# An attention and gated-MLP kernel whose order is computed by a planner: other durations, another margin and a table of priority shifts

## The chip, the cores and the metric

The kernel runs on one core of a Trainium2 chip, as one launch. The metric is the device time of that launch in microseconds (us); lower is better. Before the change it was 821.54 us, the median of three runs (820.73 to 823.94). The core's engines are called PE (matrix multiply; PEld is its weight load), ACT, DVE, POOL and SP. SP issues all the transfers (DMAs) of this kernel.

## What is computed

Attention with a causal mask and a bias from running sums, then a gated MLP (gMLP) block with a residual, for 8 batches of 576 tokens, 8 heads of 64, all in float32. `x` of the MLP is the attention's result with its heads side by side (512 wide), `w_in` is 512 x 1024, and `u` and `v` are the two halves of `h`:

```python
scores = scale * np.matmul(q, k.transpose(0, 1, 3, 2))
s_pos = np.maximum(s, 0.0)
cum = np.cumsum(s_pos, axis=-1)
bias = -(cum[:, :, :, None] - cum[:, :, None, :])
scores = np.where(causal, -1000000000.0, scores + np.minimum(bias, 0.0))
scores = scores - np.max(scores, axis=-1, keepdims=True)
attn = np.exp(scores)
attn = attn / (np.sum(attn, axis=-1, keepdims=True) + 1e-09)
return np.matmul(attn, v).astype(np.float32)
...
h = x @ w_in
c = np.float32(np.sqrt(2.0 / np.pi))
h = 0.5 * h * (1.0 + np.tanh(c * (h + 0.044715 * h ** 3)))
...
v_n = (v - mu) / np.sqrt(var + 1e-06) * g_ln
v_s = np.einsum('ts,bsd->btd', w_sg, v_n) + b_sg[None, :, None]
gated = u * v_s
return (x + gated @ w_out).astype(np.float32)
```

## The kernel before, in words

**The work.** There are 64 heads (8 per batch). A head's scores `sc` are formed on PE in five blocks of query rows. DVE adds the mask and takes the row extremes `mn` (an ISA instruction in the listings), ACT takes the exponentials into tiles `p`, PE transposes `p` into a PSUM bank `pt`, and PE multiplies the result with V into `xx` (and a 64-column rest into `x`). From head 8 on for the scores, and from head 12 on for V, each float32 operand is split into a high and a low part in a faster PE format (`pah` and `pal`, `pbh` and `pbl`, `pdh` and `pdl` for the transposed probabilities; `k`, `q`, `vs`, `xs`, `vn`, `gt` and the weights `wi`, `ws`, `wo` likewise). ACT copies the high part out of the bank, and DVE or POOL subtracts it to give the low part. After every second head the row sums are inverted (`rs`), transposed, written to DRAM (`rd`) and read back spread over the partitions (`rb`); POOL multiplies `xr` with them.

**The MLP of a batch** is cut into units: five `v` units (512 columns each, tile `vm` in PSUM; the fifth has 64 rows), eight `u` units (288 columns, `um`), eight `s` units (`sm`) and eight `o` units (`om`). A `u` unit's bank is read by the gelu: ACT, DVE, ACT, DVE in turn. A `v` unit's bank is held longer: gelu, then statistics (`bs`), then one more DVE pass into `vt`. The `vm`, `um`, `sm` and `om` tiles share three PSUM banks; `sc` has two, `pt` (with `x`) two, `xx` one. The MLP of batch b runs beside the attention of batch b+1. The last batch's MLP runs alone. The weights come in as 64-bit words and are put together from their bits during the first 150 us (`wraw`, `wbits`).

**What sets the order.** The kernel's functions emit nothing. They record each operation with a key (its place in units of one head, from the table `POS`). `graph` (L242) finds what each operation depends on. `plan` (L308) is a list scheduler: over and over it takes, of all engines, the ready operation that can start first by its assumed times, and among those of one engine that could start equally soon the one with the lowest key. Its assumed times come from `cost` (L189), from `LATENCY` per pair of engines plus `MARGIN` for each handover to an operation that depends on the result, from `OVERLAP` per engine, and from `ISSUE` per DMA on SP. `cost` also returned two flags, `wide` (DVE, operands in SBUF alone) and `lock` (POOL): the planner kept a wide DVE operation and a locking POOL operation apart in its assumed time. `emit` (L275) then writes the program, each engine's queue in exactly the planned order. On the chip an engine executes its queue strictly in that order, and waits where an operand or a buffer isn't there yet; the planned times themselves are not kept.

All instructions stand under one line of the source (L289, the call in `emit`; L362 in the changed kernel), so the views are read by tile names.

Of the kernel before, what the change touches and what calls it, by code (L numbers as in the profile page):

```python
# [10 lines left out]
F32R = mybir.dt.float32r  # L11
# [3 lines left out]
AF = mybir.ActivationFunctionType  # L15
# [10 lines left out]
CH = S // 2  # L26
# [145 lines left out]
class Program:  # L172
    def __init__(self, nc):
        self.ops, self.key, self.late, self.gate = [], 0.0, 0.0, None
        for name, n in METHODS.items():
            setattr(self, name, Engine(self, getattr(nc, name), n))
# [9 lines left out]
        return len(self.ops) - 1  # L186


    def cost(self, op):  # L189
# [5 lines left out]
        wide = lock = False  # L195
        d, load = 50.0, 0.0
        if e == PE:
            if name == "transpose":
                d, load = 110.0, 0.44 * ins[0].columns()
            else:  # L200
                w, m = ins
                load, n = 0.84 * w.columns(), m.columns()
                d = 0.463 * n if m.dtype == F32R else max(0.833 * n, load) + 0.833 * n
        elif e == ACT:
            f = kw.get("func")
            d = (195 if not any(ps) else 166) + 0.834 * n
            if f == AF.Exp:
                d = 480 + 0.834 * n
            elif f == AF.Tanh:
                d += 10  # L210
        elif e == DVE:
            d = 150 + 1.045 * n
            if name == "tensor_tensor_reduce":
                d += 7
            elif name == "reciprocal":
                d = 170
            elif name == "bn_stats":
                d = 687
            elif name == "bn_aggr":
                d = 172  # L220
            elif name == "memset":
                d = 60 + 0.8 * n
            elif n > 1 and not ops_ and not any(ps):
                wide = True
                if len(big) == 1:
                    d = 140 + 0.53 * n
        elif e == POOL:
            lock = n > 64
            if name == "tensor_tensor":
                d = (560 if kw["op"] == ALU.pow else 193) if n == 1 else 170 + 2.17 * n  # L230
            elif name == "tensor_scalar":
                d = 255 + 0.84 * n if n > 4 else 210
                if kw["op0"] == ALU.max:
                    d, lock = 3.3 * n, False
            else:
                d, lock = 140 + n, False
# [69 lines left out]


def plan(cost, pre, first, uses, order, bufs, prio, after, slack=(0, 0, 0, 0, 0), window=48):  # L308

    n = len(cost)
    left = [len(p) for p in pre]
    succ = [[] for _ in range(n)]
    for i, p in enumerate(pre):
        for q in p:
            succ[q].append(i)
    issue = [[] for _ in range(n)]
    for i, qs in after.items():  # L320
# [41 lines left out]
    held = asked = (0.0, 0.0)  # L362
    seqs = [[] for _ in range(5)]
    for _ in range(n):
        best = None
        for e in range(5):
            cand, least = [], 1e18
            for pr, i in ready[e][:window]:
                if e == PE:
                    s = max(pest + peocc, max(at[i], pest) + cost[i][2])  # L370
                    soon = pest + peocc + 1
                else:
                    s = max(at[i], free[e])
                    soon = free[e]
# [12 lines left out]
        del ready[e][bisect_left(ready[e], (pr, i))]  # L387
        _, d, load, wide, lock = cost[i]
        if e == PE:
            pest, peocc, end = s, d, s + d + 60  # L390
            free[e] = s
        elif e == SP:

            moved = max(moved, s + 1300) + d
            free[e], end = s + load, moved + 600
        else:
            if e == DVE and wide and held[0] <= s < held[1]:
                s = held[1]
            if e == POOL and lock and asked[0] <= s < asked[1]:
                s = asked[1]  # L400
            end = s + d
            if wide:
                asked = (s, end)
            if lock:
                held = (s, end)
# [20 lines left out]
def tile_attn_gmlp(  # L426
# [12 lines left out]
    nc = Program(tc.nc)  # L439
# [63 lines left out]
    sp = moe.tile([P, 5, 2, BH], F32R, name="sp", tag="vn", bufs=4)  # L503
# [61 lines left out]
    wo = const.tile([P, NC, 2, DM], F32R, name="wo")  # L565
    ws = const.tile([P, NT, 2, S], F32R, name="ws")
# [29 lines left out]
    wide = w_in.dtype != F32  # L596
# [43 lines left out]
    xr = {}  # L640
# [376 lines left out]
    sc, tr, pp = (scores, {}), (transposes, {}), (pv, {})  # L1017
# [90 lines left out]
```

## Time and profile before

| | |
|---|---|
| time, median of 3 runs | 821.54 us |
| the profiled execution's own time | 821.75 us |
| its span (first to last instruction) | 820.0 us |
| busy share PE, PEld, DVE, ACT, POOL | 96%, 84%, 75%, 70%, 61% |
| chain that ended last, by engine | PE 83%, DVE 7%, ACT 3%, DMA 3%, issue 3% |
| mean granted PE clock | 0.997 |
| DMA | 98.91 MB, 45.7% of the 16 engines' span |

The profile is of one execution. An instruction's row gives start, length, engine, operation, tiles and, in square brackets, how long the engine stood idle before it and what ended that. Matmuls are pipelined: each is shown with its whole passage, so that PE is counted as busy across small gaps. What a matmul costs PE is read from the distance between starts, as the chain view lists it (several matmuls of one tile merged, with their sum). "Busy" of DVE, ACT and POOL can be read directly.

### The profile page before, as it was taken

How to read it: one execution, taken by the hardware profiler on the slowest of the kernel's cores; microseconds unless marked ns; L12 is line 12 of the kernel's file. 1: busy time of each engine (PE TensorE's matmuls, PEld its weight loads, DVE VectorE, ACT ScalarE, POOL GpSimd, SP SyncE). 2: the span in 40 equal slices, each digit the busy share in tenths (PEclk: the TensorE clock that was granted, in tenths of full speed). 3: DMA queues.
4: the chain of work that ended last, by engine and by line, in shares of the span. 5: the costliest groups of instructions: out<-in, count | busy, mean ns of one | idle time of the engine just before them, and what ended most of it. 6: DMA issues, size and time to landing. Idle time of an engine off the chain costs nothing.

```text
span 820.0 us, 16771 instructions
## 1 busy us (share of the span) xinstructions
PE 791.2 (96%) x5129; PEld 687.4 (84%) x5129; DVE 614.2 (75%) x1845; ACT 574.1 (70%) x1576; POOL 497.2 (61%) x767
## 2 busy tenths in 40 slices
PE   7999989999999999999999999999999999999998
PEld 4455557999988998899988998889988998889998
DVE  5798489877797678875788677976788767884662
ACT  4777679867787577876687677875778866872350
POOL 3676679584467555585476745675555854746442
PEclk9999999999999999999999999999999999999999
DMA  7576754555425654354535554256443546321101
GB/s 226 160 222 164 173 158 112 128 136 141 115 65 132 165 129 117 88 137 111 148 93 130 137 128 119 68 128 170 122 120 89 138 113 152 85 51 44 43 8 59
DMA packets 75566, 98.91 MB, mean 121 GB/s; under 512 B 27298, under 2 KB 43876, under 8 KB 75476
## 3 DMA queue, kind: packets, MB, share of 16 engines
q1 hardware_dynamic: 75476, 97.84, 45.7%
q8 instruction: 41, 0.67, 0.4%
q14 instruction: 49, 0.40, 0.2%
HBM read 51.71 MB, written 9.90 MB: 75 GB/s over the span
## 4 chain that ended last, share of the span: by engine, by line
PE 83%; DVE 7%; ACT 3%; DMA 3%; issue 3%; POOL 1%; SPq 0%; ACTq 0%; POOLq 0%; DVEq 0%
PE sm L289 13%; PE om L289 13%; PE sc L289 12%; PE vm L289 12%; PE xx L289 11%; PE um L289 10%; PE pt L289 10%; DVE p L289 2%; ACT p L289 1%; DMA raw<-in_kq 1%; PE x L289 1%; DVE u L289 1%; DVE bs L289 1%; DVE vm L289 1%; DVE vt L289 1%
## 5 line engine op out<-in xcount | busy, mean ns | idle before, releaser
L289 ACT ACTIVATE p<-p,mn 128x320 f32<-128x320 f32 (+4 forms) x320 | 177.8, 557 | 42.3 <-DVE mn L289 38.9
L289 PE MATMUL pt<-ident,p 128*128 128x128 f32 x768 | 156.6, 276 | 4.7 <-ACT pal L289 1.4
L289 DVE CUSTOM_DVE_ANT_0 p<-sc,mask 128x448 f32<-128x448 f32 (+4 forms) x320 | 125.2, 421 | 25.4 <-PE sc L289 22.9
L289 PE MATMUL sc<-k,q 66*128 66x288 f32 (+9 forms) x672 | 134.5, 307 | 2.2 <-DMA k<-cum 1.3
L289 PE MATMUL sm<-ws,vn 128*128 128x288 f32 x768 | 134.2, 304 | 2.3 <-DVE u L289 2.3
L289 PE MATMUL um<-xs,wi 128*128 128x288 f32 x768 | 132.0, 306 | 1.4 <-DVE u L289 1.1
L289 PE MATMUL om<-gt,wo 128*128 128x288 f32 x768 | 131.0, 307 | 0.0
L289 PE MATMUL vm<-wi,xs 128*128 128x512 f32 (+1 forms) x416 | 126.8, 408 | 0.1
L289 PEld LDWEIGHTS pt<-ident,p 128*128 128x128 f32 x768 | 97.6, 140 | 28.5 <-issue 5.6
L289 PEld LDWEIGHTS sm<-ws,vn 128*128 128x128 f32 x768 | 112.2, 188 | 6.3 <-DVE u L289 4.9
L289 PEld LDWEIGHTS um<-xs,wi 128*128 128x128 f32 x768 | 110.7, 189 | 4.2 <-DVE vt L289 2.1
L289 PEld LDWEIGHTS sc<-k,q 128*128 128x128 f32 (+3 forms) x672 | 101.4, 181 | 13.1 <-DVE mn L289 3.7
L289 PEld LDWEIGHTS om<-gt,wo 128*128 128x128 f32 x768 | 109.3, 189 | 1.1
L289 POOL TENSOR_TENSOR k<-raw,k 128x576 fp32r<-128x576 f32 x56 | 80.3, 1434 | 32.0 <-ACT k L289 19.7
L289 POOL TENSOR_TENSOR gt<-u,gt 128x288 fp32r<-128x288 f32 x64 | 50.8, 808 | 57.9 <-ACT gt L289 55.8
L289 PEld LDWEIGHTS vm<-wi,xs 128*128 128x128 f32 (+1 forms) x416 | 71.2, 185 | 10.8 <-DVE vt L289 0.4
L289 DVE SCALAR_TENSOR_TENSOR u<-u,um 128x288 f32<-128x288 f32 x128 | 56.5, 441 | 10.5 <-ACT u L289 10.2
L289 POOL TENSOR_SCALAR bs<-bs 128x1 f32<-128x1 f32 (+1 forms) x80 | 17.2, 215 | 77.3 <-DVE bs L289 74.1
L289 ACT CAST pbh<-pt 128x512 fp32r<-128x512 f32 x104 | 49.4, 481 | 19.5 <-PE pt L289 18.5
L289 POOL TENSOR_SCALAR p<-p 64x64 f32<-64x64 f32 x128 | 32.2, 252 | 49.4 <-ACT p L289 36.7
L289 POOL TENSOR_TENSOR xr<-xr,rb 128x576 f32<-128x576 f32 x32 | 46.1, 1441 | 24.0 <-DMA rb<-rd 20.6
L289 ACT ACTIVATION_READ_ACCUMULATOR p<-p,mn 128x1 f32 (+1 forms) x320 | 60.2, 188 | 0.0
(123 smaller groups left out, 1645.5 us busy)
## 6 DMA issues: line engine op xcount, KB each, us to landing
q<-k SPq DMA_DIRECT2D x168, 144.0 KB
raw<-in_kq SPq DMA_DIRECT2D x56, 288.0 KB
vr<-in_vp SPq DMA_DIRECT2D x52, 192.0 KB
rb<-rd SPq DMA_DIRECT2D x64, 144.0 KB
out_t<-ot SPq DMA_DIRECT2D x64, 144.0 KB
k<-k SPq DMA_DIRECT2D x56, 144.0 KB
wraw<-in_w_in SPq DMA_DIRECT2D x16, 256.0 KB
kf<-in_kq SPq DMA_DIRECT2D x8, 288.0 KB
```

The lines of the kernel that those rows point to most:

```text
L289: r = getattr(op["eng"].real, op["name"])(*[f(a) for a in op["args"]], **{k: f(v) for k, v in op["kw"].items()})
```

## The change

Only the planner's assumptions and the keys change; the recorded operations are the same ones. The core of the diff:

```diff
-MARGIN = 100.0
-ISSUE = 450.0
+MARGIN = 36.0
+ISSUE = 550.0
+SHIFT = {
...
+    "act activation u 128x288 um": -6.17,
...
+    "dve tensor_tensor pal 128x512 pt": -3.4,
...
+}
 class Program:
...
+    def kind(self, op):
...
     def cost(self, op):
...
             if name == "transpose":
-                d, load = 110.0, 0.44 * ins[0].columns()
+                d, load = 110.0, 0.84 * ins[0].columns()
...
             if f == AF.Exp:
-                d = 480 + 0.834 * n
+                d, gap = 480 + 0.834 * n, -107
+            elif n == 512 and f == AF.Copy:
+                d = 715
...
             elif name == "bn_stats":
-                d = 687
+                d, gap = 687, 118
...
             elif n > 1 and not ops_ and not any(ps):
-                wide = True
-                if len(big) == 1:
-                    d = 140 + 0.53 * n
+                d = 155 + 1.62 * n if len(big) > 1 else 250 + 0.8 * n
...
-        return e, d, load, wide, lock
+        return e, d, load, gap
 def plan(...):
...
         elif e == SP:
-
+            if len(flight) >= 8:
+                s = max(s, flight[-8])
             moved = max(moved, s + 1300) + d
             free[e], end = s + load, moved + 600
+            flight.append(end + 1060)
         else:
-            if e == DVE and wide and held[0] <= s < held[1]:
-                s = held[1]
-            if e == POOL and lock and asked[0] <= s < asked[1]:
-                s = asked[1]
             end = s + d
...
-            free[e] = end - OVERLAP[e]
+            free[e] = end - OVERLAP[e] + gap
...
-    prio = [(op["key"], n) for n, op in enumerate(nc.ops)]
+    prio = [(op["key"] + SHIFT.get(nc.kind(op), 0.0), n) for n, op in enumerate(nc.ops)]
```

`kind` names an operation by engine, operation, output tile, shape and first input. `SHIFT` has 52 such names; its numbers, from -6.17 to 4.5, are added to the key, and one unit is one head. `gap` lengthens or shortens the time for which an engine is taken. `flight` lets the planner's SP wait for the eighth DMA before.

What this does to the queues is shown at three places. The numbers in names such as `k_5862` are buffer numbers.

**Place 1: PE, batch 3, where its first `sm` matmuls stand.** `xx<-pah` needs the high part `pah`, which ACT copies from the bank that the last `pt` of `p_3`, `p_2`, `p_1` and `p_4` filled. Before:

```order
L289 MATMUL um<-xs,wi 128x288 x7
L289 MATMUL sc<-k_5862,q_5872 128x448
L289 MATMUL sc<-k_5876,q_0_90 128x448
L289 MATMUL sc<-k_5862,q_5872 64x64
L289 MATMUL sc<-k_5876,q_0_90 64x64
L289 MATMUL pt<-ident,p_4_255 128x128 x2
L289 MATMUL sc<-k_5862,q_5872 128x320
L289 MATMUL sc<-k_5876,q_0_90 128x320
L289 MATMUL sc<-k_5862,q_5872 128x192
L289 MATMUL sc<-k_5876,q_0_90 128x192
L289 MATMUL xx<-pah,vs 128x512
L289 MATMUL sm<-ws,vn 128x288 x4
```

Now, at the same place, where the first of the two `p_3` transposes ends the first bank:

```order
L362 MATMUL pt<-ident,p_3_129 128x128 x2
L362 MATMUL pt<-ident,p_2_126 128x128
L362 MATMUL pt<-ident,p_4_276 128x128
L362 MATMUL um<-xs,wi 128x288 x11
L362 MATMUL pt<-ident,p_2_126 128x128
L362 MATMUL pt<-ident,p_4_276 128x128
L362 MATMUL um<-xs,wi 128x288
L362 MATMUL sc<-k_5832,q_5851 128x288
L362 MATMUL sc<-k_5844,q_0_90 128x288
L362 MATMUL pt<-ident,p_3_129 128x128
L362 MATMUL pt<-ident,p_4_276 128x128
L362 MATMUL xx<-pah,vs 128x512
```

Twelve `um` matmuls, two `sc` and seven transposes stand between the bank's end and its use, where one transpose and four `sc` stood.

**Place 1 on DVE**, beside those matmuls. `pal` and `pbl` belong to attention; `vt`, `vm` and `bs` with 64 rows are the fifth `v` unit; `u` is gelu. Before:

```order
L289 RECIPROCAL rs<-rs 128x10
L289 SCALAR_TENSOR_TENSOR vt<-vt,vm 64x512
L289 SCALAR_TENSOR_TENSOR u_6005<-u_6005,um 128x288
L289 ISA p_3_124,mn<-sc,mask 64x64
L289 ISA mn 64x1
L289 TENSOR_TENSOR pal<-pt,pah 128x512
L289 TENSOR_TENSOR pbl<-pt,pbh 128x512
L289 SCALAR_TENSOR_TENSOR vm<-vt,vm 64x512
L289 SCALAR_TENSOR_TENSOR u_6072<-u_6072,um 128x288
L289 BN_STATS bs<-vm 64x6
L289 TENSOR_TENSOR pbl<-pt,pbh 128x256
L289 TENSOR_TENSOR pdh<-pt,pdh 64x64 x2
```

Now:

```order
L362 TENSOR_TENSOR pal<-pt,pah 128x512
L362 TENSOR_TENSOR pbl<-pt,pbh 128x512
L362 TENSOR_TENSOR vm<-vm,vt 64x512
L362 ISA p_4_198,mn<-sc,mask 128x288
L362 ISA mn 128x1
L362 SCALAR_TENSOR_TENSOR u_6085<-u_6085,um 128x288
L362 TENSOR_TENSOR pbl<-pt,pbh 128x256
L362 ISA p_2_120,mn<-sc,mask_86 128x320
L362 ISA mn 128x1
L362 SCALAR_TENSOR_TENSOR vt<-vt,vm 64x512
L362 SCALAR_TENSOR_TENSOR u_6085<-u_6085,um 128x288
L362 TENSOR_TENSOR pdh<-pt,pdh 64x64 x2
```

`pal`, both `pbl` and `pdh` stood among the fifth `v` unit's passes, with `bs` ahead of the last of them; now `pal` and `pbl` stand ahead of that unit's first pass, and its statistics behind `pdh`.

**Place 2: PE, some 10 us later in the same batch**, where the next `sm` unit needs a bank that a `um` unit (12 matmuls) has to give back. Before:

```order
L289 MATMUL um<-xs,wi 128x288 x4
L289 MATMUL pt<-ident,p_2_122 128x128
L289 MATMUL sc<-k_5862,q_5872 128x288
L289 MATMUL sc<-k_5876,q_0_90 128x288
L289 MATMUL um<-xs,wi 128x288 x7
L289 MATMUL pt<-ident,p_1_196 128x128
L289 MATMUL um<-xs,wi 128x288 x3
L289 MATMUL pt<-ident,p_2_122 128x128
L289 MATMUL um<-xs,wi 128x288
L289 MATMUL pt<-ident,p_4_198 128x128 x2
L289 MATMUL sm<-ws,vn 128x288 x5
```

Now:

```order
L362 MATMUL sc<-k_5991,q_6007 128x192
L362 MATMUL sc<-k_6005,q_1_101 128x192
L362 MATMUL um<-xs,wi 128x288 x10
L362 MATMUL pt<-ident,p_2_120 128x128
L362 MATMUL pt<-ident,p_4_198 128x128
L362 MATMUL um<-xs,wi 128x288 x2
L362 MATMUL xx<-pah,vs 128x512
L362 MATMUL xx<-pal,vs 128x512
L362 MATMUL xx<-pbh,vs 128x448
L362 MATMUL pt<-ident,p_3_122 128x128
L362 MATMUL pt<-ident,p_4_198 128x128
L362 MATMUL sm<-ws,vn 128x288 x3
```

Before, the `um` unit whose bank `sm` takes ended within the first row shown; now it ended ahead of all these rows, and the twelve `um` in them are a unit of their own.

**Place 3: SP, during the first 100 us**, where the next head's `raw` (K and Q) is fetched among weights (`wraw`, 256 KB each). Before:

```order
L289 DMA rb<-rd 64x576 x2
L289 DMA wraw<-in_w_out 128x512
L289 DMA xq<-xs 128x2x64 x2
L289 DMA wraw<-in_w_out 128x512 x3
L289 DMA q_1103<-k_1079 64x576
L289 DMA q_0_90<-k_1079 64x576
L289 DMA raw<-in_kq 128x576
```

Now:

```order
L362 DMA rb<-rd 64x576 x2
L362 DMA wr_972<-bh 1x16x18 x2
L362 DMA q_1058<-k_1041 64x576
L362 DMA q_0_90<-k_1041 64x576
L362 DMA wraw<-in_w_out 128x512
L362 DMA raw<-in_kq 128x576
L362 DMA q_1058<-k_1054 64x576
L362 DMA wst<-in_w_sgt 64x288
L362 DMA wraw<-in_w_out 128x512 x2
```

`raw` stood behind four `wraw`, three of them in a row; now one `wraw` stands ahead of it, and the pair follows it.

More of the change, by code (lines that the diff above doesn't have):

```diff
@@ L63 @@
 PE, ACT, DVE, POOL, SP = range(5)
+UNITS = ("pe", "act", "dve", "pool", "sp")
 METHODS = {"tensor": PE, "scalar": ACT, "vector": DVE, "gpsimd": POOL, "sync": SP}
@@ L67 @@
 OVERLAP = [0, 93, 75, 25, 0]
-MARGIN = 100.0
-ISSUE = 450.0
+MARGIN = 36.0
+ISSUE = 550.0
+SHIFT = {
+    "act activation p__ 128x192 p__": 3.23,
+    "act activation p__ 128x320 p__": 1.06,
+    "act activation p__ 128x576 p__": 1.07,
+    "act activation p__ 64x64 p__": 0.73,
+    "act activation u 128x288 um": -6.17,
+    "act activation wbits 128x256 wraw": -1.92,
+    "act copy k 128x576 raw": 3.54,
+    "act copy pah 128x512 pt": -2.55,
+    "act copy pal 128x512 pt": -1.51,
+    "act copy pdh 64x64 pt": 0.17,
+    "act copy vs 128x384 vr": 1.01,
+    "act copy xr 64x64 x": -0.9,
+    "dve bn_aggr bs 128x2 bs": -1.68,
+    "dve bn_stats bs 64x6 vm": 0.81,
+    "dve scalar_tensor_tensor u 128x288 u": -2.54,
+    "dve scalar_tensor_tensor vm 128x512 vt": 0.46,
+    "dve scalar_tensor_tensor vt 128x512 vt": -0.33,
+    "dve scalar_tensor_tensor vt 64x512 vt": -1.36,
+    "dve tensor_scalar wbits 128x256 wbits": -1.69,
+    "dve tensor_tensor pal 128x512 pt": -3.4,
+    "dve tensor_tensor pdl 128x192 pt": 1.12,
+    "dve tensor_tensor vm 64x512 vm": 0.64,
+    "dve tensor_tensor ws 128x288 wst": -1.4,
+    "dve tensor_tensor xr 64x64 x": 4.5,
+    "dve tensor_tensor_reduce p__ 128x192 sc": -0.27,
+    "dve tensor_tensor_reduce p__ 128x320 sc": 1.08,
+    "dve tensor_tensor_reduce p__ 64x64 sc": -5.74,
+    "pe matmul sc 128x192 q": -1.11,
+    "pe matmul sc 128x192 q_": -4.69,
+    "pe matmul sc 128x288 qf": 0.07,
+    "pe matmul sc 128x320 q": -0.05,
+    "pe matmul sc 128x320 q_": -0.69,
+    "pe matmul sc 128x448 q": -1.38,
+    "pe matmul sc 128x448 q_": -0.36,
+    "pe matmul sc 128x448 qf": -1.38,
+    "pe matmul sc 64x64 q": -0.2,
+    "pe matmul sm 128x288 vn": 0.36,
+    "pe matmul vm 128x512 xq": 0.63,
+    "pe matmul vm 128x512 xs": -0.09,
+    "pe matmul vm 64x512 xs": 0.54,
+    "pe matmul x 64x64 vf": -2.06,
+    "pe matmul xx 128x512 vs": 1.01,
+    "pe matmul xx 64x448 vf": 1.38,
+    "pe matmul xx 64x512 vf": 1.7,
+    "pool tensor_scalar wbits 128x256 wbits": 0.96,
+    "pool tensor_scalar xs 128x576 xr": -0.78,
+    "pool tensor_tensor k 128x576 raw": -1.91,
+    "pool tensor_tensor wo 128x256 wbits": 2.47,
+    "sp dma_start wraw 128x512 -": -0.25,
+    "sp dma_start wst 128x288 -": 0.87,
+    "sp dma_start wst 64x288 -": 0.87,
+    "sp dma_start xq 128x128 xs": 1.08,
+}
 class Buf:
@@ L186, in add, with name @@
         return len(self.ops) - 1
+    def kind(self, op):
+        def name(vs):
+            return "".join(c for c in vs[0].buf.name if not c.isdigit()) if vs else "-"
+        vs = op["outs"] + op["ins"]
+        dims = "%dx%d" % (vs[0].dims[0][1], vs[0].columns())
+        return " ".join([UNITS[op["eng"].n], op["name"], name(op["outs"]), dims, name(op["ins"])])
     def cost(self, op):
@@ L194, in cost @@
         ops_ = bool(outs) and outs[0].buf.pool.psum
-        wide = lock = False
-        d, load = 50.0, 0.0
+        d, load, gap = 50.0, 0.0, 0.0
         if e == PE:
             if name == "transpose":
-                d, load = 110.0, 0.44 * ins[0].columns()
+                d, load = 110.0, 0.84 * ins[0].columns()
             else:
@@ L202, in cost @@
                 load, n = 0.84 * w.columns(), m.columns()
-                d = 0.463 * n if m.dtype == F32R else max(0.833 * n, load) + 0.833 * n
+                d = 0.463 * n if m.dtype == F32R else max(0.84 * n, load) + 0.84 * n + 70
         elif e == ACT:
@@ L206, in cost @@
             d = (195 if not any(ps) else 166) + 0.834 * n
+            rows = (outs or big)[0].dims[0][1]
             if f == AF.Exp:
-                d = 480 + 0.834 * n
+                d, gap = 480 + 0.834 * n, -107
+            elif n == 512 and f == AF.Copy:
+                d = 715
+            elif n == 384:
+                gap = 115
+            elif rows == 64 and f is None:
+                gap = 95 if n == 64 else 45
             elif f == AF.Tanh:
@@ L212, in cost @@
             d = 150 + 1.045 * n
+            rows = (outs or big)[0].dims[0][1]
+            if name == "tensor_tensor" and rows == 64:
+                gap = 98 if n == 64 else 79
+            elif name == "scalar_tensor_tensor" and n == 512:
+                gap = 48
             if name == "tensor_tensor_reduce":
                 d += 7
+                gap = 60 if n == CH else 0
             elif name == "reciprocal":
-                d = 170
+                d = 202
             elif name == "bn_stats":
-                d = 687
+                d, gap = 687, 118
             elif name == "bn_aggr":
@@ L233, in cost @@
                 if kw["op0"] == ALU.max:
-                    d, lock = 3.3 * n, False
+                    d = 3.3 * n
             else:
-                d, lock = 140 + n, False
+                d = 140 + n
         else:
@@ L361, in plan @@
     pest = peocc = moved = 0.0
-    held = asked = (0.0, 0.0)
+    flight = []
     seqs = [[] for _ in range(5)]
@@ L387, in plan @@
         del ready[e][bisect_left(ready[e], (pr, i))]
-        _, d, load, wide, lock = cost[i]
+        _, d, load, gap = cost[i]
         if e == PE:
@@ L392, in plan @@
         elif e == SP:
+            if len(flight) >= 8:
+                s = max(s, flight[-8])
             moved = max(moved, s + 1300) + d
             free[e], end = s + load, moved + 600
+            flight.append(end + 1060)
         else:
-            if e == DVE and wide and held[0] <= s < held[1]:
-                s = held[1]
-            if e == POOL and lock and asked[0] <= s < asked[1]:
-                s = asked[1]
             end = s + d
[L402 to L405, printed above, removed]
-            free[e] = end - OVERLAP[e]
+            free[e] = end - OVERLAP[e] + gap
         start[i], fin[i] = s, end
```

1 line of the change is left out of this document (removed).

## Prediction

> **What bounds the kernel now.** I read the page first: busy shares, then the chain that ended last.
>
> ```profile
> PE 791.2 (96%) x5129; PEld 687.4 (84%) x5129; DVE 614.2 (75%) x1845; ACT 574.1 (70%) x1576; POOL 497.2 (61%) x767
> PE 83%; DVE 7%; ACT 3%; DMA 3%; issue 3%; POOL 1%; SPq 0%; ACTq 0%; POOLq 0%; DVEq 0%
> ```
>
> PE is the bound, and it has work almost everywhere. But matmuls overlap, so "busy" hides small gaps. The chain view gives what a matmul costs PE where nothing is waited for, and how long a batch takes.
>
> ```profile
> 72.67 0.45 PE pt L289 x4
> 284.90 1.08 PE sc L289 x8
> ...
> 666.87 1.08 PE sc L289 x8
> ...
> 770.03 2.79 PE vm L289 x12
> 772.83 3.20 PE um L289 x24
> 805.64 11.09 PE om L289 x84
> ```
>
> The same group of eight `sc` matmuls comes back once a batch, at 284.90 and, four batches on, at 666.87: a batch takes 95.5 us. A 288-column matmul costs 3.20/24 = 0.133 us (0.46 ns a column), a 512-column one 2.79/12 = 0.233, a transpose 0.45/4 = 0.113.
>
> One batch therefore needs, counted from the loops: 96 `um` + 96 `om` + 112 `sm` matmuls at 0.133 = 40.4 us; 56 `vm` at 0.233 = 13.0; 100 transposes at 0.113 = 11.3; for eight heads' scores eight narrow matmuls (1.08) and four of 288 columns (0.53), 12.9; for eight heads' `xx` and `x` 3072 columns each at 0.46 ns, 11.3. The sum is 88.9 us. So **6.6 us of each batch are lost in waits**, and 88.9 us is a floor that no order changes, as long as PE runs the same matmuls.
>
> Where are they lost? The windows of one batch show it, columns being PE, PEld, DVE, ACT, POOL:
>
> ```profile
> 412.00:420.00 8.00, 8.00 (x50) 6.91 (x49) 7.14 (x21) 6.92 (x20) 5.74 (x12) 1.00 0.32 82
> 420.00:428.00 8.00, 7.96 (x55) 7.04 (x54) 7.60 (x26) 6.84 (x20) 6.13 (x15) 1.00 0.42 95
> 428.00:436.00 8.00, 7.22 (x47) 5.89 (x47) 7.27 (x21) 6.84 (x20) 3.67 (x7) 1.00 0.10 25
> 460.00:468.00 8.00, 8.00 (x60) 7.81 (x59) 3.95 (x11) 4.14 (x11) 5.12 (x6) 1.00 0.79 226
> ```
>
> From 412 to 436 us DVE is busy for 22.0 of 24 us; at 460 it is half idle. In this bulge gelu, the `v` units' statistics and the softmax meet, and there PE loses time. The timeline of PE, and the chain inside the bulge:
>
> ```profile
> 429.44 0.75 PE L289 MATMUL sc<-k,q 128*128 128x320 f32 x4
> 430.78 0.50 PE L289 MATMUL xx<-pah,vs 128*128 128x512 f32 x1 [0.59 <-ACT pah L289]
> ...
> 435.82 0.90 PE L289 MATMUL um<-xs,wi 128*128 128x288 f32 x5
> ...
> 438.00 0.27 PE L289 MATMUL pt<-ident,p 128*128 128x128 f32 x1
> ...
> 441.05 0.93 PE L289 MATMUL sm<-ws,vn 128*128 128x288 f32 x5 [0.38 <-DVE u L289]
> ```
>
> ```profile
> 429.45 0.62 DVE p L289
> ...
> 434.85 0.36 DVE pdl L289
> ```
>
> **Place 1**, from 429.44 to 435.82, takes 6.38 us. PE runs 8128 columns of matmuls there (3.74 us) and five transposes (0.57): 2.1 us are lost. The chain runs on DVE throughout, from `p` to `pdl`. **Place 2**, from 438.00 to 441.05, takes 3.05 us for 13 matmuls of 288 columns (1.73) and five transposes (0.57): 0.75 us lost, while `sm` waits for a bank that gelu's last pass releases. These two make 2.85 of the 6.6 us.
>
> The other loss is at the start. In windows of 20 us:
>
> ```profile
> 0.00:20.00 20.00, 14.45 (x53) 9.48 (x53) 10.97 (x40) 9.25 (x26) 7.25 (x19) 1.00 0.74 229
> 80.00:100.00 20.00, 18.16 (x86) 10.91 (x86) 8.43 (x35) 12.92 (x40) 14.41 (x20) 0.91 0.72 179
> 120.00:140.00 20.00, 18.15 (x116) 14.34 (x115) 18.04 (x54) 18.78 (x51) 18.65 (x34) 1.00 0.38 90
> sum 200.00, PE 184.00 PEld 132.64 DVE 151.81 ACT 143.79 POOL 133.98; mean PE 18.40 PEld 13.26 DVE 15.18 ACT 14.38 POOL 13.40
> ```
>
> PE idles 16.0 of the first 200 us, 5.55 of them in the first 20, where it has no data yet. The remaining 10.45 us are open to a better order.
>
> **The change, part by part.** No operation is added or removed, so PE's floor stays. But lone transposes become runs, so both have to be priced. A lone one among `um` matmuls:
>
> ```profile
> 438.54 1.08 PE L289 MATMUL um<-xs,wi 128*128 128x288 f32 x7
> 439.46 0.27 PE L289 MATMUL pt<-ident,p 128*128 128x128 f32 x1
> 439.49 0.64 PE L289 MATMUL um<-xs,wi 128*128 128x288 f32 x3
> 439.97 0.27 PE L289 MATMUL pt<-ident,p 128*128 128x128 f32 x1
> ```
>
> The next `um` starts 0.03 us after it, which looks free; but the three `um` then take 0.48 us to the next transpose, 0.08 more than 3 x 0.133. Together 0.11, what a transpose in a run costs. Runs cost 0; with 800 transposes and an error of 2 ns each, 1.6 us either way.
>
> *Place 1.* The cover of `pah` is the PE work between the bank's last transpose and `xx<-pah`. Before, it is one transpose and 1024 columns, 0.58 us. Now it is twelve `um` (1.60), two `sc` (0.27) and seven transposes (0.79): 2.65 us.
>
> ```profile
> L289 ACT CAST pah<-pt 128x512 fp32r<-128x512 f32 x52 | 30.3, 583 | 13.4 <-PE pt L289 7.7 <-PE xx L289 5.5
> L289 DVE TENSOR_TENSOR pal<-pt,pah 128x512 fp32r<-128x512 f32 x52 | 35.7, 687 | 4.4 <-ACT pah L289 3.7
> ```
>
> `pah` takes 0.58 us and `pal` 0.69, so the old cover couldn't hold even an idle ACT; the new one holds both in a row. With `pal`, `pbl` and `pdh` ahead of the statistics, I take the loss here to fall from 2.1 to about 0.2. *Place 2.* Before, the bank's `um` unit ended 12 matmuls of 288 columns, two `sc` and five transposes ahead of `sm`, 2.4 us. Now the rows shown alone hold 2.9 us, and the unit ended earlier still. I take all 0.75 as gone. *The rest*, 3.75 us a batch, hangs on many short handovers; for a tenth of it, 0.35 us, the longer covers should help as well. In sum 3.0 us a batch. Its bounds: 0.75 (place 2 alone, if the bulge of place 1 only moves), and 5.1 (a rest of 1.5). From 200 to 750 us the batch repeats 550/95.5 = 5.76 times: **17.3 us**, between 4.3 and 29. After 750 us the last MLP runs alone and both orders end in a row of 84 `om`; 0.
>
> *The start.* What is late at 95 us is a fetch:
>
> ```profile
> 95.46 6.99 DMA raw<-in_kq
> ...
> 97.52 0.44 ACT L289 ACTIVATE wbits<-wraw 128x256 f32<-128x256 f32 x1 [2.87 <-DMA wraw<-in_w_out]
> ...
> 102.52 0.67 ACT L289 CAST k<-raw 128x576 fp32r<-128x576 f32 x1 [1.37 <-DMA raw<-in_kq]
> ```
>
> ```profile
> L289 PE MATMUL om<-gt,wo x768: 288/295/384, 168.0 to 816.4; 128*128 128x288 f32 x192
> ```
>
> `raw` took 7 us behind the burst of `wraw`, and ACT stood 2.87 and 1.37 us. With `raw` ahead of the burst this goes, but then a `wraw` is late, for `wo`, which the first `om` needs at 168 us (its row stands last above). Elsewhere in the start DVE is full (18.04 of 20 at 120 us), and an order can't shorten that. Of 10.45 us I take half, **5 us**; bounds 0 and 9.
>
> *Margin, issue, flight.* They show only through the order, and are in the above. On SP, `rb` now follows `rd` directly in 12 of 32 cases, in none before:
>
> ```profile
> 483.05 0.29 SPq L289 DMA_DIRECT2D rd<-rt  x1
> ...
> 486.73 1.19 SPq L289 DMA_DIRECT2D rb<-rd  x2
> ```
>
> Before, 3.7 us lay between, filled with other issues. Now SP waits for `rd` to land, up to 3.7 us, with `q`, `k` and `raw` of the next head queued behind it, and POOL's `xr` behind `rb`. I take 0, since the heads' splits stand 9 us of PE work or more ahead of their scores; if half of the 12 cost PE 1.5 us, 9 us. The Trainium skill, page "DMA: Bandwidth & Descriptors", section "Anatomy of one DMA — SWDGE (gpsimd) path", gives a fixed 2.0 us for a transfer, on another issuing path. By that, as an estimate, SP would stand 12 x 2 = 24 us in all; if PE lost every one of them, the sum below would end at 823. No row here shows the landing by itself.
>
> **Sum.** 17.3 + 5 = 22.3 us. The profiled execution took 821.75 us (span 820.0, and 1.75 around it), so 799.4; the median lies 0.2 lower, and I say **799**.
>
> **Rivals.**
>
> *The bulge moves (A).* DVE's work from 412 to 436 us is the same, and so is its 92% share; what is put ahead pushes something else behind, here the fifth `v` unit, on which later `sm` wait. Then place 2 alone is won, 4.3 us: 817. For it speaks the full DVE; against it, that DVE is half idle at 460 us and has time to catch up.
>
> *Nothing happens (B).* The waits at these places last 0.59 and 0.38 us of PE idle time by the timeline; if the 6.6 us are mostly delays that no order touches, the table moves names and not time: 820. Against it, 2.85 us sit at two places with a named cause.
>
> *Nearly all is won (C).* If 5.1 us a batch go and 9 at the start, 38 us: 783.
>
> *Slower (D): DVE and POOL collide at the start.* The old planner kept `wide` DVE and `lock` POOL operations apart; the new one doesn't, and uses mean durations.
>
> ```profile
> L289 DVE SCALAR_TENSOR_TENSOR wbits<-wraw,wbits x48: 407/423/1778, 15.2 to 150.2; 128x256 int32<-128x256 int32 x48
> L289 DVE SCALAR_TENSOR_TENSOR wbits<-wraw,wbits 128x256 int32<-128x256 int32 x48 | 27.3, 573 | 0.4
> 60.74 1.78 DVE L289 SCALAR_TENSOR_TENSOR wbits<-wraw,wbits 128x256 int32<-128x256 int32 x1
> 60.88 0.72 POOL L289 TENSOR_TENSOR wi<-wbits,wi 128x256 fp32r<-128x256 f32 x1
> ```
>
> The same operation takes 0.42 us in the median and up to 1.78, beside POOL's work; its mean is 0.57. So 48 of them lose 48 x 0.15 = 7.2 us already. With the 32 other SBUF operations of the start, 80 in all, a mean loss of 0.6 us instead of 0.15 would be 36 us of a full DVE; less the 17 us of the batches the time is 840. It decides above 0.43 us each (22.3 us in all plus what is lost now). The page "SBUF — State Buffer" of the Trainium skill, section "SBUF: two separate sides", says that DVE and GpSimd share a port pair as an exclusive lock, the loser blocked for the other's whole instruction; the row of 1.78 us agrees. By that rule each unplanned meeting costs up to one POOL operation. Against it, POOL's work is as thin as before, and the old order had meetings too.
>
> **How the numbers follow.** Forecast (790 to 811): 0.55. C (under 790): 0.10. A (812 to 817): 0.12. B: 0.14. D: 0.09. A measurement of this kernel can tell about 0.5% (4 us) from no change: faster than 817.4 are forecast, C and A, 0.77; same 0.14; slower 0.09. The range, 783 to 820, reaches over A to the middle of B, and leaves out D and the tails of B and C, under 0.2.
>
> **What would show it.** The same `sc` group should come back every 92.5 us. `xx<-pah` in the middle of a batch should show no idle time, and the idle time of PE before 200 us should be near 11. If a batch takes 94.5 us or more with a DVE chain of several us in it, A was right; if the median of the `wbits` passes rises, D. I am wrong as well if transposes in runs cost more than 0.113 us, as the floor would then rise.

## The result, and the profile after

The changed kernel takes **796.62 us** (median of 4 runs, 795.22 to 797.55), beside 822.01 us for the kernel before (820.73 to 823.94): a ratio of **0.9688, 95% interval 0.9662 to 0.9714**. The profiled execution of it took 797.55 us, with a span of 795.7, 24.3 less than before. 799 was forecast, with the range 783 to 820.

The page of the changed kernel, busy shares and the chain that ended last:

```profile
PE 778.5 (98%) x5129; PEld 689.7 (87%) x5129; DVE 616.9 (78%) x1845; ACT 576.5 (72%) x1576; POOL 492.5 (62%) x767
PE 89%; DVE 4%; ACT 2%; issue 2%; DMA 2%; POOL 1%; SPq 0%; DVEq 0%; POOLq 0%; ACTq 0%
```

PE's share of the chain rose from 83 to 89%, and DVE's fell from 7 to 4%. The busy time of DVE, ACT and POOL is within 1% of what it was. Windows of 8 us in one batch (columns PE, PEld, DVE, ACT, POOL) and one of 200 us in the middle of the kernel; the last row is that of the kernel before:

```profile
412.00:420.00 8.00, 8.00 (x55) 7.08 (x54) 7.59 (x29) 7.89 (x23) 5.65 (x10) 1.00 0.29 74
420.00:428.00 8.00, 8.00 (x61) 7.80 (x60) 7.73 (x25) 7.89 (x24) 4.57 (x10) 1.00 0.40 100
428.00:436.00 8.00, 8.00 (x62) 7.76 (x61) 7.75 (x23) 5.99 (x17) 3.43 (x9) 1.00 0.60 174
...
400.00:600.00 200.00, 199.55 (x1379) 185.99 (x1378) 163.12 (x503) 158.28 (x433) 126.29 (x196) 1.00 0.46 124
```

```profile
400.00:600.00 200.00, 196.87 (x1334) 179.24 (x1333) 155.45 (x478) 150.81 (x413) 120.13 (x184) 1.00 0.47 121
```

The bulge is still there: from 412 to 436 us DVE is busy for 23.1 of 24 us, more than the 22.0 before. But PE shows no idle time in it any more, and idles 0.45 us in 200, where 3.13 were.

For the batch period I take an operation that runs once a batch, DVE's last pass over the fifth `v` unit. First the timeline of the kernel before, then of the changed one, third and sixth batch:

```profile
346.88 0.69 DVE L289 TENSOR_TENSOR vnr<-vt,vnr 64x512 fp32r<-64x512 f32 x1
...
633.39 0.69 DVE L289 TENSOR_TENSOR vnr<-vt,vnr 64x512 fp32r<-64x512 f32 x1
```

```profile
341.77 0.69 DVE L362 TENSOR_TENSOR vnr<-vt,vnr 64x512 fp32r<-64x512 f32 x1
...
616.95 0.69 DVE L362 TENSOR_TENSOR vnr<-vt,vnr 64x512 fp32r<-64x512 f32 x1
```

A batch took (633.39 - 346.88)/3 = 95.5 us, and takes 91.7 now (91.6 from the fourth on). The same rows of all eight batches place the gain: at the second, 251.28 and 248.50, the changed kernel is 2.8 us ahead; between the second and the eighth (794.36 and 769.92) it wins 21.7; behind the eighth it loses 0.1. Together 24.3, the difference of the spans.

Place 1 of the prediction now reads so, on PE:

```profile
419.32 0.60 PE L362 MATMUL pt<-ident,p 128*128 128x128 f32 x4
419.68 1.71 PE L362 MATMUL um<-xs,wi 128*128 128x288 f32 x11
...
421.99 0.48 PE L362 MATMUL xx<-pah,vs 128*128 128x512 f32 x1
...
427.31 0.29 PE L362 MATMUL sm<-ws,vn 128*128 128x288 f32 x1
```

`xx<-pah` shows no idle time ahead of it. From 419.32 to 427.31, 7.99 us, PE runs 39 matmuls of 288 columns (5.19 us at 0.133), 3520 columns of `xx`, `x` and one `sc` (1.63) and nine transposes (1.02), by the rows between: 7.84 us. So 0.15 us are lost there, where 2.1 were. On DVE beside it, `pal` and `pbl` stand ahead of the fifth `v` unit, as in the order:

```profile
420.23 0.68 DVE L362 TENSOR_TENSOR pal<-pt,pah 128x512 fp32r<-128x512 f32 x1
420.83 0.67 DVE L362 TENSOR_TENSOR pbl<-pt,pbh 128x512 fp32r<-128x512 f32 x1
421.43 0.68 DVE L362 TENSOR_TENSOR vm<-vm,vt 64x512 f32<-64x512 f32 x1
...
426.63 0.68 DVE L362 BATCH_NORM_STATS2 bs<-vm 64x6 f32<-64x512 f32 x1
```

For place 2, the group of `sm` matmuls in one batch, before (442.3 to 537.9 us) and now (433.7 to 525.3). The last number is PE's idle time ahead of the group, and what ended it:

```profile
L289 PE MATMUL sm<-ws,vn 128*128 128x288 f32 x98 | 17.9, 306 | 0.4 <-DVE u L289 0.4
```

```profile
L362 PE MATMUL sm<-ws,vn 128*128 128x288 f32 x97 | 17.4, 303 | 0.0
```

In the start the gain came at another place than forecast. Three windows of 20 us of the changed kernel, and then the one of the kernel before that the prediction does not show:

```profile
80.00:100.00 20.00, 18.82 (x91) 12.17 (x92) 13.20 (x40) 13.56 (x41) 14.44 (x18) 0.91 0.66 172
120.00:140.00 20.00, 20.00 (x129) 16.35 (x128) 18.63 (x54) 18.41 (x51) 16.60 (x29) 1.00 0.44 118
140.00:160.00 20.00, 20.00 (x149) 19.19 (x148) 19.01 (x62) 17.35 (x50) 14.80 (x23) 1.00 0.48 120
```

```profile
140.00:160.00 20.00, 18.09 (x131) 16.83 (x130) 18.44 (x53) 16.72 (x49) 12.68 (x20) 1.00 0.50 125
```

From 120 to 160 us PE idled 3.76 us before and not at all now, although DVE is fuller there than it was. From 80 to 120 us, where `raw` was late, PE's idle time fell only from 3.6 to 2.9 us.

### The profile page after: what moved, and what is told of

The parts are those of the page before. It is cut to its first block, busy times and chain, and to the rows that moved or that the text cites. A ratio compares the mean times of both kernels' runs of the same rounds, so it can differ in the third digit from the quotient of the medians.

```text
span 795.7 us, 16803 instructions
## 1 busy us (share of the span) xinstructions
PE 778.5 (98%) x5129; PEld 689.7 (87%) x5129; DVE 616.9 (78%) x1845; ACT 576.5 (72%) x1576; POOL 492.5 (62%) x767
## 4 chain that ended last, share of the span: by engine, by line
PE 89%; DVE 4%; ACT 2%; issue 2%; DMA 2%; POOL 1%; SPq 0%; DVEq 0%; POOLq 0%; ACTq 0%
PE sm L362 15%; PE um L362 13%; PE sc L362 13%; PE xx L362 12%; PE om L362 12%; PE vm L362 12%; PE pt L362 11%; PE x L362 1%; DVE wbits L362 1%; ACT p L362 1%; DMA wraw<-in_w_in 1%; DMA k<-cum 1%; DVE p L362 1%; ACT pdh L362 0%; SPq L362 0%
## 5 line engine op out<-in xcount | busy, mean ns | idle before, releaser
L362 ACT ACTIVATE p<-p,mn 64x64 f32<-64x64 f32 (+4 forms) x320 | 178.7, 559 | 55.7 <-DVE mn L362 53.2
L362 DVE CUSTOM_DVE_ANT_0 p<-sc,mask 128x320 f32<-128x320 f32 (+4 forms) x320 | 126.0, 421 | 23.8 <-PE sc L362 21.5
L362 PE MATMUL sc<-k,q 128*128 128x288 f32 (+9 forms) x672 | 140.7, 307 | 1.3 <-DVE mn L362 1.1
L362 PE MATMUL pt<-ident,p 128*128 128x128 f32 x768 | 137.1, 275 | 3.2 <-DVE pbh L362 1.5
L362 PE MATMUL om<-gt,wo 128*128 128x288 f32 x768 | 132.9, 304 | 0.0
L362 PE MATMUL um<-xs,wi 128*128 128x288 f32 x768 | 129.7, 302 | 0.0
L362 PE MATMUL vm<-wi,xs 128*128 128x512 f32 (+1 forms) x416 | 119.5, 405 | 0.0
L362 POOL TENSOR_TENSOR vs<-vr,vs 128x384 fp32r<-128x384 f32 x52 | 53.0, 1020 | 20.2 <-ACT vs L362 16.1
L362 DVE TENSOR_TENSOR pbl<-pt,pbh 128x512 fp32r<-128x512 f32 x104 | 56.4, 546 | 6.3 <-ACT pbh L362 5.6
```

The source lines that it names most:

```text
L362: r = getattr(op["eng"].real, op["name"])(*[f(a) for a in op["args"]], **{k: f(v) for k, v in op["kw"].items()})
```

## The experiments

The theory that I started from (T): the table makes the gain, by longer covers at the handovers of the bulge. Its rivals: the durations and the margin make it (P), or the table is worth something only on the new durations (M, later N). For the start, where only 2.8 of the forecast 5 us came, they are that DVE and POOL collide (C), or that transfers hold the start (Q). "Second batch" and "period" are read from the `vnr` row as above, in the profiled execution; ratios are to the kernel before, with 95% intervals. "Clock" is the mean granted PE clock of each kernel's executions, from the lowest to the highest. "Half clock" is the time ahead of the second batch, in the profiled execution, for which that clock stood at 0.5.

| kernel | time, us | ratio | second batch at | period | clock | half clock, us |
|---|---|---|---|---|---|---|
| before | 822.0 | 1 | 251.28 | 95.5 | 0.997 to 1.0 | 3.4 |
| changed | 796.62 | 0.9688 (0.9662 to 0.9714) | 248.50 | 91.7 | 0.998 to 1.0 | 3.4 |
| no table | 823.87 | 1.0018 (0.9994 to 1.0042) | 246.07 | 96.2 | 0.994 to 1.0 | 0 |
| table alone | 822.05 | 0.9993 (0.9974 to 1.0012) | 257.55 | 94.0 | 0.994 to 0.998 | 6.8 |
| margin 100 | 801.02 | 0.9748 (0.9725 to 0.9772) | 253.18 | 91.9 | 0.996 to 0.998 | 6.8 |
| old durations | 838.03 | 1.0202 (1.0177 to 1.0228) | 259.54 | 96.5 | 0.983 to 0.995 | 3.4 |
| before, margin 36 | 837.41 | 1.0190 (1.0173 to 1.0207) | 255.51 | 97.7 | 0.994 to 0.996 | 10.2 |
| without `pah`, `pal` entries | 812.47 | 0.9886 (0.9855 to 0.9917) | 254.08 | 94.1 | 0.992 to 0.996 | 10.2 |
| `pah`, `pal` entries alone | 830.63 | 1.0100 (1.0071 to 1.0129) | 253.84 | 96.2 | 0.990 to 0.994 | 10.2 |
| without `u` entries | 814.84 | 0.9912 (0.9884 to 0.9941) | 250.00 | 94.3 | 0.992 to 1.0 | 0 |
| apartness kept | 802.91 | 0.9761 (0.9742 to 0.9781) | 252.54 | 91.7 | 0.996 to 1.0 | 0 |
| without weight entries | 798.98 | 0.9720 (0.9700 to 0.9740) | 249.75 | 91.6 | 0.998 | 3.4 |
| `wo` later | 802.87 | 0.9757 (0.9732 to 0.9782) | 249.17 | 91.8 | 0.996 to 1.0 | 0 |
| table from head 12 on | 795.85 | 0.9674 (0.9657 to 0.9692) | 246.85 | 91.6 | 0.998 to 1.0 | 0 |

The last two columns matter for the reading. In the changed kernel's trace, for instance, the granted clock is 0.50 from 82.3 to 85.7 us:

```profile
82.30:85.70 3.40, 3.40 (x8) 1.23 (x7) 0.20 (x1) 0.12 (x1) 0.84 (x1) 0.50 0.49 130
```

Each such stretch of 3.4 us can cost up to 1.7 us. The kernel before and the changed one have one each ahead of the second batch, so their difference of 2.8 us there is untouched. The starts of kernels with none or with more of them can differ by 1.7 us a stretch for this reason alone. The times have such a share, too. An estimate of it, at most, is the time multiplied by what the mean clock lacks to 1: some 10 us of the 838.03, 7 of the 830.63, 4 of the 837.41 and of the 812.47, 3 of the table alone and 2 of no table. The periods hold no such stretch, but for old durations (one; a batch without it takes 96.1). What lowers the clock no run here shows.

### The table taken out, and the table alone

```diff
-SHIFT = {
-    "act activation p__ 128x192 p__": 3.23,
...
-}
+SHIFT = {}
```

> The changed kernel with an empty table: the new durations, margin, issue time and flight limit stay. Theory T (the table carries the gain, by longer covers on PE's handovers): the batch period goes back to 94 to 96 us and the time to 812 to 824. Rival P (the durations and the margin carry it, the table is a trimming): period at most 92.5 us, time at most 803. Rival M (both are needed in part): 804 to 811.

No gain is left, as T expected, though the parts differ. The start is 5.2 us faster than before (246.07), of which up to 1.7 are the clock. The batches are 0.7 us slower each (96.2), so that 2.1 us of the lead are left at the eighth, and behind that 1.7 more go. Rival P falls.

The other way round, `SHIFT`, `kind` and the line with `prio` put into the kernel before:

> The kernel before with the table alone: old durations, margin 100, issue 450, and the old apartness of DVE and POOL. Theory T: most of the gain is there, period 91.5 to 93 us, time 797 to 806. Rival P: period 95 us or more, time 815 to 824. Rival M (the table was fitted to the new durations and is of little use without them): 806 to 815.

Nothing either, so T falls too: the time is that of P's range, the period (94.0) in nobody's. The start loses 6.3 us, up to 1.7 of them to the clock, and a batch gains 1.5. In the batch from 352.9 to 446 us `xx<-pah` still waits as in the kernel before, so the table by itself doesn't make the cover of place 1:

```profile
L353 PE MATMUL xx<-pah,vs 128*128 128x512 f32 x8 | 3.6, 450 | 0.6 <-ACT pah L353 0.6
```

The chain of waits of the same batch names transfers, which that of the changed kernel doesn't, but PE hardly stands for them: the transfer of 5.42 us ends in an idle time of 0.31.

```profile
438.29 5.42 DMA k<-k
```

```profile
443.84 0.45 PE L353 MATMUL sc<-k,q 128*128 128x448 f32 x1 [0.31 <-DMA k<-k]
```

M is what remains: the table and the new assumptions win 25 us together and, by the times, nothing each (at full clock, by the estimate above, the table alone some 3). Which of the new assumptions the table needs is narrowed down below, but not to one: the issue time and the flight limit were never tried by themselves.

### The margin, in both planners

```diff
-MARGIN = 36.0
+MARGIN = 100.0
```

> The changed kernel with the old margin of 100 ns. Theory T: the margin only shows through the order, and a larger one leaves as much cover: 792 to 801, period 91 to 92.5 us. Rival P: the smaller margin is what lets the planner pack, so the time rises to 804 or more, period 93 us or more.

801.02 us, 4.4 more than the changed kernel, at the edge of T's range. The period is the same within 0.2 us, so in a batch of the middle the margin is worth nothing, as T said. The profiled executions differ by 5.5 us. At the second batch the one with margin 100 is 4.7 us late (253.18 against 248.50), up to 1.7 of them by the clock. By the seventh 2.9 are left, and some 3 more are lost on the way to the eighth (775.87 against 769.92). So the difference stands at the start and in the last batch.

Then the margin of 36 with the old durations, with the table and the new issue time and flight limit (`cost` as before, `gap` 0, no apartness):

> The changed kernel with the old planner's durations (no gap, weight load of a transpose 0.44 ns a column); table, margin, issue time and flight limit as changed, and no apartness. Theory N (the table works only on the order that the new durations give; margin 100 and the apartness in a batch cost nothing): the batch gain falls to under 2 us, as with the table alone, time 806 to 818. Rival (issue time and flight limit are what the table alone lacked): batch gain 3.5 us or more, time 796 to 803.

838.03 us, slower than the kernel before, and outside both expectations: I had not thought that the small margin would hurt. By the trace 8.3 us are lost ahead of the second batch (259.54), and a batch without half clock takes 96.1 us, 2.1 more than with the table alone and its margin of 100. Up to 10 us of the 16 above the kernel before can be the clock. From this came the last test, the kernel before with the margin alone:

```diff
-MARGIN = 100.0
+MARGIN = 36.0
```

> The kernel before with the margin of 36 ns alone. Theory N (the old durations are too short for DVE's passes between SBUF tiles, and the margin of 100 made up for it; a small margin is usable only with the longer durations): slower, 828 to 842, as the kernel with table and margin 36 on old durations was (838). Rival (a small margin does harm only together with the table, or none at all): 818 to 825.

837.41, in N's range, and a batch takes 97.7 us, 2.2 more. The same edit thus costs 15.4 us on the old durations (up to 4 of them by the clock) and wins 4.4 on the new ones with the table. This fits that the large margin had covered what the old durations left out, but no run shows which durations these were. The diff names candidates: among others, `gap` adds 118 ns behind each `bn_stats` and 98 and 79 ns behind passes of 64 rows, which is 5 x 0.118 + 8 x (0.098 + 0.079) = 2.0 us of DVE a batch for the `v` units and the two `xr` passes of each head. The new durations were not tried one by one.

### Which entries of the table

The entries of place 1 taken out, then these entries alone, in the changed kernel:

```diff
-    "act copy pah 128x512 pt": -2.55,
-    "act copy pal 128x512 pt": -1.51,
-    "dve tensor_tensor pal 128x512 pt": -3.4,
```

> The changed kernel without the table's three entries for the copies and differences pah and pal (-2.55, -1.51, -3.4). If those entries make the cover of place 1, its 2.1 us of loss come back: period 93.3 us or more, time 806 to 812. If the cover comes from the other entries and durations (transposes and softmax earlier), the period stays within 0.7 us of 91.6 and the time is 795 to 801.

> The changed kernel with the table cut to its three entries for pah and pal. If place 1 alone is the gain and these entries are enough for it (2.6 us a batch were lost without them): period near 93, time 806 to 811. If they work only together with the entries that move transposes, gelu and scores: period 94.5 us or more, time 816 to 825.

Without them 2.4 us of the 3.8 us of a batch are lost; alone they win nothing in a batch (96.2, as with no table). But the loss is not at place 1. In the groups of one batch of each, the kernel before (442.3 to 537.9 us) and the changed kernel without these entries (440.6 to 534.8); the last numbers are PE's idle time ahead of the group:

```profile
L289 PE MATMUL xx<-pah,vs 128*128 128x512 f32 x8 | 3.3, 407 | 0.6 <-ACT pah L289 0.6
```

```profile
L359 PE MATMUL xx<-pah,vs 128*128 128x512 f32 x8 | 3.3, 411 | 0.0
```

`xx<-pah` still does not wait. The time came out half a microsecond above what the first theory expected, but its reason is wrong. What came back has no single name: as an estimate from the distances between PE's starts, waits that the trace names in this batch (for `mn`, `p` and `vn` among others) make about half of it, and small delays that no wait explains the rest. Alone, at 830.63, the entries make the kernel slower than either expectation, though up to 7 us of it can be the clock. Then gelu's two entries were taken out:

```diff
-    "act activation u 128x288 um": -6.17,
-    "dve scalar_tensor_tensor u 128x288 u": -2.54,
```

> The changed kernel without the table's two entries for gelu's passes that read or follow um (ACT -6.17, DVE -2.54). If they make the earlier return of the banks at place 2 (0.75 us a batch): period 92.1 to 92.6 us, time 799 to 803. If the banks come back early enough without them: period 91.6, time 795 to 798. If gelu's priority orders far more than place 2: 806 or more.

814.84, the third of the expected cases: 2.5 us a batch, and again not at the place that I had named. No `sm` waits for gelu. The timeline of PE in a batch shows `x` waiting for `pdh`, for 1.2 us in the batch from 437.9 to 532.2 us:

```profile
451.39 0.27 PE L360 MATMUL x<-pdh,vs 128*128 128x64 f32 x1 [0.30 <-DVE pdh L360]
458.45 0.27 PE L360 MATMUL x<-pdh,vs 128*128 128x64 f32 x1 [0.27 <-DVE pdh L360]
```

The entries' losses, 2.4 and 2.5, add up to more than the 3.8 of the whole, so they are not prices of single places.

### The start: collisions, transfers, and the table itself

The old apartness of `wide` and `lock` operations put back:

> The changed kernel with the old planner's apartness of wide DVE and locking POOL operations put back. Theory C (collisions are what the start lost: the wbits, ws and shift passes of DVE took 5.2 us longer in sum): those passes fall back to means of 0.57, 0.83 and 0.47 us and the time falls by 2 to 5 us, to 792 to 795. Rival (DVE isn't what ends last there, or the planner's times are too far from the chip's to keep them apart): means within 5% of those of the changed kernel, time 795 to 801.

The groups of the first 200 us, mean ns of one last, in the changed kernel and then in this one:

```profile
L362 DVE SCALAR_TENSOR_TENSOR wbits<-wraw,wbits 128x256 int32<-128x256 int32 x48 | 28.1, 604 | 0.2
L362 DVE TENSOR_SCALAR wbits<-wbits 128x256 int32<-128x256 int32 x24 | 13.2, 552 | 2.7 <-POOL wbits L362 2.6
L362 DVE TENSOR_TENSOR ws<-wst,ws 128x288 fp32r<-128x288 f32 x8 | 8.2, 1035 | 0.8 <-ACT ws L362 0.6
```

```profile
L365 DVE SCALAR_TENSOR_TENSOR wbits<-wraw,wbits 128x256 int32<-128x256 int32 x48 | 26.0, 561 | 0.1
L365 DVE TENSOR_SCALAR wbits<-wbits 128x256 int32<-128x256 int32 x24 | 13.0, 541 | 2.6 <-POOL wbits L365 2.5
L365 DVE TENSOR_TENSOR ws<-wst,ws 128x288 fp32r<-128x288 f32 x8 | 6.4, 827 | 2.1 <-ACT ws L365 2.0
```

The passes get shorter by 48 x 0.043 + 24 x 0.011 + 8 x 0.208 = 4.0 us, two of the three to the means that C wanted, and the kernel gets 6.3 us slower, more than the rival said. In the profiled execution the span is 799.3 us, 3.6 longer, and the second batch is already 4.0 late, with no half clock ahead of it. C falls as the price of the start. The edit moves the order as well, so what the collisions cost by themselves isn't measured. Then the table's eight entries for the weights (`wraw`, `wbits`, `wst`, `ws`, `wo`) were taken out:

> The changed kernel without the table's eight entries for the weights' operations (wraw, wbits, wst, ws, wo), which run before 175 us alone. If they are what cost the start 3 us against the kernel without a table: 792 to 795, with the period unchanged at 91.6. If it is the entries for k, the softmax or gelu: 795 to 800. If they help the start: 800 or more.

Here the three groups take 566, 387 and 764 ns, 8.0 us less in sum, and the time is 2.4 us longer, the second of the expected cases; the intervals of the two kernels overlap. So shorter passes of DVE did not make the start faster in either run. Their chains show a transfer of over 5 us at the same point, near 95 us. Each is shown with the matmul that it released: first the changed kernel, then the one with apartness, then the one without the weight entries.

```profile
98.88 5.49 DMA k<-cum
```

```profile
104.50 0.90 PE L362 MATMUL sc<-k,q 66*128 66x320 f32 x6 [0.17 <-DMA k<-cum]
```

```profile
96.98 5.46 DMA k<-k
```

```profile
102.57 0.44 PE L365 MATMUL sc<-k,q 128*128 128x448 f32 x1 [0.62 <-DMA k<-k]
```

```profile
93.59 5.18 DMA k<-k
```

```profile
98.91 0.74 PE L354 MATMUL sc<-k,q 128*128 128x448 f32 x4 [0.57 <-DMA k<-k]
```

The 5 us are the transfer's own length. PE ran other matmuls meanwhile and stood only 0.17, 0.62 and 0.57 us, so this step of the chain is no measure of what PE lost, and the wait of about 5 us in the next expectation is not one of PE.

Was it the burst of weights for `w_out` that made the transfer late? Its keys were moved:

```diff
-           wu=(7.0, 10.0), ws=(9.0, 11.0), wo=(11.0, 14.0), f0=2.0, f1=9.6)
+           wu=(7.0, 10.0), ws=(9.0, 11.0), wo=(13.0, 16.0), f0=2.0, f1=9.6)
```

> The changed kernel with w_out's loads and splits given keys 13 to 16 instead of 11 to 14, so that they come some 20 us later, behind the stretch from 80 to 110 us in which every kernel so far shows a wait of about 5 us for a transfer. Theory Q (the bursts of transfers there cap the start, and a better order only gives the wait another name): no wait of over 2 us for a transfer between 80 and 110 us, 3 to 5 us won, 792 to 794. Rival (another transfer or DVE is late there just the same): 795 to 800.

```profile
96.96 5.37 DMA k<-cum
```

```profile
102.46 0.90 PE L362 MATMUL sc<-k,q 66*128 66x320 f32 x6 [0.21 <-DMA k<-cum]
```

The transfer is as long as before, and the kernel is 6.2 us slower, more than the rival said; its profiled execution, the fastest of the four, is 2.3 us slower than the changed kernel's. Q falls: the transfer did not get shorter, and PE stood 0.21 us for it. The transfers in question belong to a head's split (K and Q copied across partitions), and in the code the split of one head can only start when an earlier head has given back its tiles. Whether that sets their 5 us stays open.

Last, the table for keys from 12 on alone, so that the start is planned with the new durations only:

```diff
-    prio = [(op["key"] + SHIFT.get(nc.kind(op), 0.0), n) for n, op in enumerate(nc.ops)]
+    prio = [(op["key"] + (SHIFT.get(nc.kind(op), 0.0) if op["key"] >= 12 else 0.0), n) for n, op in enumerate(nc.ops)]
```

> The changed kernel with the table's shifts only for operations whose key is 12 or more, so that the start is ordered by the new durations alone and the batches by both. By the comparison of matmuls done at equal times, the kernel without the table was 5 us ahead of the kernel before at 240 us, the changed one 2. Theory T2 (start and batches add up: durations win the start, the table costs 3 us there and wins the batches): 792 to 795, period 91.6. Rival (the start ends in another state for which the table's batches aren't fitted, or the seam costs what it gains): 796 to 802.

At the second batch it is 1.65 us ahead of the changed kernel, and the period is the same; the time, 795.85, lies 0.8 us under the changed kernel's, which the two intervals don't separate, and between T2's range and the rival's. It is the fastest that I found. That the table costs in the start is not shown by it: the lead of 1.65 us is what the changed kernel's half clock can account for, 1.7. The same holds for 1.7 of the 2.4 us by which the kernel without a table is ahead at its second batch (246.07). Its row from 80 to 100 us has the full clock, where the changed kernel's, above, has 0.91:

```profile
80.00:100.00 20.00, 18.03 (x91) 11.31 (x91) 10.86 (x37) 13.42 (x40) 12.38 (x16) 1.00 0.85 206
```

And PE idles more there than with the table, 13.7 us of the first 200 against 12.15.

## Why the prediction was right, and where it was not

**The bound.** Right. The matmuls stayed and PE's waits went; 2.7 us a batch are left above the floor of 88.9.

**Place 1.** 2.1 to 0.2 us was forecast, 2.1 to 0.15 measured. The row of `xx<-pah` and DVE's order are as described.

**Place 2.** Right: PE's idle time ahead of the `sm` matmuls of a batch went from 0.4 us, ended by gelu, to 0.0. The price of 0.75 us has no row of its own.

**"The rest", 0.35 us a batch: mis-sized.** From the fourth on a batch won 3.9 us instead of 3.0 (95.5 to 91.6), so the rest gave 3.9 - 1.95 - 0.75 = 1.2. Against the floor the excess is 6.6 us before and 2.7 after. As an estimate, from the distances between the starts of successive matmuls in one batch of each trace, the waits for `pah` fell from 0.8 to 0, those for gelu from 0.7 to 0, and those for `pdl` from 0.8 to 0.4. The other 2.0 are short handovers and, for about half, small delays that no wait explains. I had put nine tenths of the rest down as out of reach of the order; about a third of it wasn't.

**The sum of the batches** was 17.3, of 5.76 batches at 3.0; it became 21.7 in the six from the second to the eighth, 3.6 each, since the first two of them won only 2.3 and 3.5.

**The start, 5 us: mis-sized, and not won where I said.** 2.8 us came by the second batch. My step was that `raw` ahead of the burst takes the wait at 95 us away, and that elsewhere DVE is full and "an order can't shorten that". The windows show something else: from 80 to 120 us PE's idle time fell by 0.7 us, and from 120 to 160 us, where DVE was full, by 3.8; in the first 60 us it rose by 1.2. So the second half of the step is wrong, and that half of 10.45 came near the measured 3.85 us of idle time is luck. What took the idle time from 120 to 160 us away, be it a late effect of `raw` or another part of the order, was not tested. The prediction's row from 80 to 100 us also has a clock of 0.91 that it doesn't price: a half clock of 3.4 us, which both traces have. The two errors in size, 4.4 us too little for the batches and 2.2 too much for the start, offset each other in part, with 799 for 796.6.

PE's idle time before 200 us was to be near 11:

```profile
sum 200.00, PE 187.85 PEld 137.06 DVE 158.28 ACT 146.28 POOL 133.10; mean PE 18.78 PEld 13.71 DVE 15.83 ACT 14.63 POOL 13.31
```

It is 12.15, from 16.0.

**Margin and flight, "in the above": too short.** That they show only through the order is right; that the order needs them was not seen. The prediction priced two places by what stands there and never asked which edit puts it there. The runs answer: not the table alone, and not the new assumptions alone; each of these comes out within 2 us of the kernel before.

**`rd` and `rb`, 0 with up to 9:** right. POOL's wait for `rb` grew from 9.6 to 14.5 us, and PE did not feel it (0.45 us of idle time in 200). Groups from 200 to 750 us, first before, then after:

```profile
L289 POOL TENSOR_TENSOR xr<-xr,rb 128x576 f32<-128x576 f32 x23 | 33.2, 1443 | 10.7 <-DMA rb<-rd 9.6 <-DVE ot L289 0.9
```

```profile
L362 POOL TENSOR_TENSOR xr<-xr,rb 128x576 f32<-128x576 f32 x24 | 34.4, 1434 | 30.7 <-DMA rb<-rd 14.5 <-DVE mn L362 5.6 <-DMA k<-cum 4.2
```

**Rivals.** A fell: DVE is fuller in the bulge, and PE doesn't wait behind it. B and C fell by the time. D had its mechanism (DVE was 6.5 us busier before 200 us, the mean of `ws` rose from 825 to 1035 ns) but not its price: two runs with shorter passes were no faster. The sign that I gave for it, the median of the `wbits` passes, did not move (423 and 419 ns). Its estimate that a meeting costs up to one POOL operation is too low by its own row: the pass of 1.78 us lost 1.36, and the POOL operation shown beside it took 0.72 and the next one 0.67.

## What to carry to other kernels

A list scheduler's durations, its margin and its priorities are one setting: here a table that won 25 us with the new assumptions was worth next to nothing with the old ones, so they are changed and measured together. A place in the profile where the bound engine waits tells what can be won, but removing the entry that seems to serve it may move the loss elsewhere; price the whole period, and count the short handovers too. A transfer of 5 us on the chain is not 5 us lost: read how long the bound engine stood behind it, here 0.17 us. And look at the granted clock before two starts are compared to within some microseconds.

## What the hardware showed that was not expected

A transfer of 4.5 KB (`k<-cum`) took 5.49 us from its issue, in a stretch of the start where the transfers of weights and heads were mixed. The Trainium skill, page "DMA: Bandwidth & Descriptors", section "Anatomy of one DMA — SWDGE (gpsimd) path", gives 2.0 us as the fixed part of one, on another issuing path; this row is far above it, and no run here shows how much of it was queueing.

The loss by DVE and POOL working at once is real. In the changed kernel's trace 9 of the 48 `wbits<-wraw,wbits` passes ran while POOL did nothing, and none of them took more than 0.43 us; the 39 beside POOL's work took 0.65 us in the mean and up to 2.73. The two orders with less of this loss were no faster at the end of the kernel.
